# Attention quotients of two tiles at a time: four banks, one chain of VectorE operations per pair

## The chip, the cores and the metric

The kernel runs on one core of one Trainium2 chip. A core has TensorE (matmuls, PE in the profile), VectorE (DVE), ScalarE (ACT), GpSimd (POOL) and a queue for transfers on SyncE (SP). The engines run side by side and wait for each other through semaphores. PSUM, where matmuls put their results, is laid out by this kernel as eight banks. The metric is device time in microseconds (us), the median of several runs.

## The reference

It is a transformer block on 2048 rows of 448 features: a linear attention with 16 heads of 28 features, then a gated MLP.

```python
h  = x + A(layernorm(x));  h2 = h + B(layernorm(h))
# A, per head: phi(u) = [softmax(u @ w_phi), softmax(-u @ w_phi)]
kv  = einsum("bhsf,bhsd->bhfd", phi_k, v);  z = einsum("bhsf->bhf", phi_k)
num = einsum("bhqf,bhfd->bhqd", phi_q, kv)
den = einsum("bhqf,bhf->bhq", phi_q, z)[..., None] + 1e-6
o   = num / den                          # "the quotient"; then o @ wo
# B: (sigmoid(x @ w_gate) * (x @ w_up)) @ w_down
```

## The kernel before

The rows are 16 tiles of 128. A graph records every operation with what it reads and writes; ORDER lists, per engine, the order of the queue, and PROGRAM the order in which operations that share a bank follow one another. Semaphores are derived from both: a bank is written again only after the last reader of what it held. So a change of ORDER changes no arithmetic, only who waits for whom.

The quotient is worked by `num`. It already takes `n` tiles and a first bank `b`; each tile needs two banks. The kernel before always calls it with one tile.

```python
def num(t, n=1, b=6):
    s, NB = t % NS, 2 * n
    ...                                   # 16 small matmuls per tile into banks b, b+1, ...
    rsm = reciprocal(OM[..., E-1])        # VectorE, 16 numbers per row and tile
    qq  = rsm * OP[..., E-1]              # VectorE
    b   = OM[..., 0:EV] * qq              # VectorE, 464 numbers per tile, from PSUM
    c   = b + OP[..., 0:EV]               # VectorE, 464 numbers per tile, from PSUM
    den = 1e-6 * OP[..., E-1] + c[..., EV-1]   # VectorE, last reader of the banks
    rden = reciprocal(den)                # VectorE
    for each tile: o = c * rden           # GpSimd or VectorE, by ORDER; then a transpose
...
# kvz: the masked kv sums. Its columns of ones are copied beforehand, by VectorE or ScalarE, by ORDER:
cp(kvz[:, 0:2, ...] , maskK[...])         # 128 rows, 16 numbers, fp32 to bf16
for a, half in ((0, LO), (1, HI)):
    cp(kvz[half, 2, ...], maskK[half, a, ...])   # 64 rows, 8 numbers, twice
...                                       # whole code: cut here
```

(The code of `num` is abridged to its arithmetic; names are the kernel's. Others that come up below: phi of k is worked by ss (sums), rs (their reciprocals) and phi (the multiplication); v1 copies v out of PSUM; pq are the projections of q and eq their exps; oT is a quotient transposed, oTe its copy out of PSUM; h is the first residual sum, hn its layernorm, hT its transpose and hTe the copy of that which the gate matmuls, ga and gb, read; hh is the gated product. A number behind a name is the tile.)

The softmax here doesn't subtract the row's maximum and nothing guards it: scores larger than these inputs give would overflow.

## Time and profile before

| | before |
|---|---|
| median of three runs | 205.57 us |
| span of the profiled run | 203.7 us |
| TensorE busy | 97% of the span |
| VectorE busy | 67% |
| start of the first quotient matmul | 46.20 us |
| start of the first gate matmul | 61.01 us |

A line of a timeline reads: start, duration, engine, line of the code, operation, output and inputs, shapes, count, and in brackets how long the engine had been idle and what ended that. The stage at issue lies between the last two rows of the table: projections of q (with their exps on ScalarE), quotients, output projection and second layernorm of the first tiles, until the gate matmuls can start. After that TensorE runs nearly without holes to the end.

### The profile page before, as it was taken

How to read it: one execution, taken by the hardware profiler on the slowest of the kernel's cores; microseconds unless marked ns; L12 is line 12 of the kernel's file. 1: busy time of each engine (PE TensorE's matmuls, PEld its weight loads, DVE VectorE, ACT ScalarE, POOL GpSimd, SP SyncE). 2: the span in 40 equal slices, each digit the busy share in tenths (PEclk: the TensorE clock that was granted, in tenths of full speed). 3: DMA queues.
4: the chain of work that ended last, by engine and by line, in shares of the span. 5: the costliest groups of instructions: out<-in, count | busy, mean ns of one | idle time of the engine just before them, and what ended most of it. 6: DMA issues, size and time to landing. Idle time of an engine off the chain costs nothing.

```text
span 203.7 us, 5834 instructions
## 1 busy us (share of the span) xinstructions
PE 196.7 (97%) x2474; PEld 111.6 (55%) x2474; DVE 135.9 (67%) x340; ACT 97.4 (48%) x195; POOL 57.9 (28%) x98
## 2 busy tenths in 40 slices
PE   7899999999979999999999999999999999999995
PEld 3744556655448876777444544444555555554443
DVE  5899999978799988677668967526532422262224
ACT  2889999889892544522333343323522222222220
POOL 4699999942345310400023020001400000000000
PEclk9999999999999999999999999999999999999999
DMA  6975633899522371240004511040212000004002
GB/s 163 306 139 122 77 73 66 282 295 352 141 52 55 55 100 27 55 81 0 3 0 80 119 30 28 2 77 24 56 36 60 3 0 3 0 0 138 0 0 90
DMA packets 32866, 16.25 MB, mean 80 GB/s; under 512 B 25096, under 2 KB 31944, under 8 KB 32840
## 3 DMA queue, kind: packets, MB, share of 16 engines
q1 hardware_dynamic: 32336, 15.86, 33.2%
q8 instruction: 19, 0.31, 0.7%
q10 hardware_dynamic: 504, 0.03, 0.2%
q14 instruction: 7, 0.06, 0.1%
HBM read 8.34 MB, written 1.84 MB: 50 GB/s over the span
## 4 chain that ended last, share of the span: by engine, by line
PE 89%; DVE 4%; ACT 3%; DMA 1%; issue 1%; POOL 0%; DVEq 0%
PE psum L296 82%; PE psum L852 5%; DVE st L499 2%; DMA x_sb<-in_A_x_dram 1%; ACT eq L653 1%; ACT eq L652 1%; PE psum L567 1%; ACT junk L756 1%; ACT x_sb L748 1%; PE psum L492 1%; DVE kvz L683 1%; DVE mv L500 0%; DVE b_sb L717 0%; DVE c_sb L720 0%; POOL rst L512 0%
## 5 line engine op out<-in xcount | busy, mean ns | idle before, releaser
L296 PE MATMUL psum<-xnT,wg_sb 64*128 64x512 bf16 (+1 forms) x490 | 93.3, 333 | 0.4 <-ACT eq L653 0.2
L296 PE MATMUL psum<-xnT,wu_sb 64*128 64x512 bf16 (+1 forms) x490 | 93.0, 333 | 0.0
L824 ACT ACTIVATE sg_sb<-psum 128x512 bf16<-128x512 f32 (+1 forms) x70 | 35.0, 512 | 89.6 <-PE psum L296 89.0
L825 DVE SCALAR_TENSOR_TENSOR hhT<-sg_sb,psum 128x512 bf16<-128x512 bf16 (+1 forms) x70 | 39.0, 577 | 52.5 <-ACT sg_sb L824 52.1
L296 PEld LDWEIGHTS psum<-xnT,wg_sb 64*128 64x128 bf16 x490 | 44.3, 94 | 22.9 <-DVE hhT L825 4.8
L296 PEld LDWEIGHTS psum<-xnT,wu_sb 64*128 64x128 bf16 x490 | 44.3, 94 | 13.0
L296 PE MATMUL psum<-wd_sb,hhT 64*128 64x448 bf16 x336 | 36.9, 349 | 0.0
L296 PEld LDWEIGHTS psum<-wd_sb,hhT 64*128 64x128 bf16 x336 | 17.3, 94 | 14.8 <-DVE x_sb L751 0.6
L622 POOL TENSOR_TENSOR phi<-hhT,rs 128x896 bf16<-128x896 bf16 x14 | 24.1, 1738 | 0.9 <-PE psum L296 0.8
L296 PE MATMUL psum<-Wk,xnT 64*128 64x448 bf16 x112 | 22.3, 350 | 0.2
L296 PE MATMUL psum<-wv_sb,xnT 64*128 64x448 bf16 x112 | 22.4, 351 | 0.1
L759 POOL TENSOR_SCALAR ve<-ssq 128x1 f32<-128x1 f32 x16 | 3.1, 192 | 66.1 <-ACT junk L756 65.7
L618 DVE TENSOR_REDUCE ss<-hhT 128x32 f32<-128x896 bf16 x16 | 17.0, 1062 | 0.7 <-ACT hhT L615 0.7
L296 PE MATMUL psum<-xnT,Wq 64*120 64x512 bf16 x112 | 15.0, 385 | 0.1
L729 POOL TENSOR_TENSOR o_pad<-c_sb,rden 128x448 bf16<-128x448 bf16 x10 | 9.3, 936 | 15.6 <-DVE rden L725 13.4
L296 PE MATMUL psum<-wo_o,oT 64*128 64x448 bf16 x56 | 13.2, 350 | 0.0
L296 PE MATMUL psum<-wo_e,oT 64*128 64x448 bf16 x56 | 13.1, 349 | 0.0
L756 ACT ACTIVATE junk<-x_sb,nm 128x448 bf16<-128x448 bf16 x16 | 10.6, 661 | 1.9 <-DVE nm L754 1.8
L852 PE MATMUL psum<-wd_sb,hhT 128*128 128x448 bf16 (+2 forms) x70 | 11.1, 316 | 0.0
L859 DVE SCALAR_TENSOR_TENSOR x_sb<-psum,x_sb 128x448 bf16<-128x448 f32 (+2 forms) x17 | 9.4, 591 | 2.1 <-PE psum L852 1.6
L499 DVE BATCH_NORM_STATS2 st<-x_sb 128x6 f32<-128x448 bf16 x16 | 9.4, 611 | 1.9 <-DMA x_sb<-in_A_x_dram 1.9
L296 PEld LDWEIGHTS psum<-Wk,xnT 64*128 64x128 bf16 x112 | 7.6, 94 | 5.3 <-ACT hhT L615 0.7
(87 smaller groups left out, 240.3 us busy)
## 6 DMA issues: line engine op xcount, KB each, us to landing
out_dram<-x_sb SPq DMA_DIRECT2D x15, 112.0 KB, 1.8
x_sb<-in_A_x_dram SPq DMA_DIRECT2D x7, 224.0 KB, 4.5
wd_sb<-in_B_w_down_dram SPq DMA_DIRECT2D x7, 224.0 KB, 9.3
wg_sb<-in_B_w_gate_dram SPq DMA_DIRECT2D x3, 448.0 KB, 8.2
wu_sb<-in_B_w_up_dram SPq DMA_DIRECT2D x3, 448.0 KB, 6.9
wv_sb<-in_A_wqkv_dram SPq DMA_DIRECT2D x2, 224.0 KB, 5.0
wk_sb<-in_A_wqkv_dram SPq DMA_DIRECT2D x2, 196.0 KB, 3.3
wo_e<-in_A_wo_dram SPq DMA_DIRECT2D x1, 336.0 KB, 7.9
```

The source lines that it names most:

```text
L296: p = e.matmul(o, lhsT=w, rhs=r, start=st, stop=sp, tile_position=(row, 0))
L492: p = e.transpose(ps[:, kt * P:(kt + 1) * P], src, ident[:])
L499: op("dve", "bst%d" % t, lambda e: e.bn_stats(st1[:, t, :], x_sb[:, t, :]), r=[("x", t)], w=[("st1", t)])
L618: op("dve", "ss%d" % t, lambda e: e.tensor_reduce(ss[:, s, :], eks, AX.X, ALU.add), r=[("ek", s)], w=[("ss", s)])
L622: return e.tensor_tensor(phi[:, sp, :, :, :].rearrange("p b a n -> p (b a) n")[:, :, 0:56].rearrange("p b (h d) -> p b h d", h=2), eks.rea ...
L729: return e.tensor_tensor(o_pad[:, t % NO, off:off + D].rearrange("p (h d) -> p h d", h=H), c_sb[:, t % NS, :, 0:DH], rden[:, t % NS, :][:, ...
L756: op("act", "sq%d" % t, lambda e: e.activation(junk[:, t % 2, :], h_sb[:, t, :], ACT.Square, bias=nm2[:, t:t + 1], accum_out=ssq2[:, t:t + ...
L759: op("pool", "ve%d" % t, lambda e: e.tensor_scalar(ve2[:, t:t + 1], ssq2[:, t:t + 1], 1.0 / D, EPS, op0=ALU.mult, op1=ALU.add), r=[("ssq2" ...
L824: op("act", "sig" + nm, lambda e: e.activation(sg_sb[:, k, 0:N], bk(bg)[:, 0:N], ACT.Tanh, scale=0.5), r=[B(bg)], w=[("sg", k)])
L825: op("dve", "hh" + nm, lambda e: e.scalar_tensor_tensor(out=hhT[(t0 // 4) % NHH][:, ff, ns], in0=sg_sb[:, k, 0:N], scalar=1.0, in1=bk(bu)[ ...
L852: p = e.matmul(bk(b)[:, lo:hi], lhsT=hb[:, ff, TS(t)], rhs=wd_sb[:, ff, lo:hi], start=ff == 0, stop=ff == FT - 1)
L859: op("dve", "fin%d%s" % (t, nm), lambda e: e.scalar_tensor_tensor(out=h_sb[:, t, lo:hi], in0=bk(b)[:, lo:hi], scalar=0.5, in1=h_sb[:, t, l ...
```

## The change

The intent: an operation has a fixed cost; one operation over two tiles pays it once. So tiles 0 and 1 become one pair, tiles 2 and 3 another. A pair takes four banks in a row, 4 to 7, so the projections that used 4 and 5 have to go elsewhere. The queues were then put in a new order around this. The core of the diff:

```diff
 PROGRAM = (
-    "pq:0,0,4 pq:0,1,4 kvz pq:1,0,0 pq:1,1,4 pq:2,0,0 num:0 num:1,1,2 ot:0 ot:1 wo:0 pq:2,1,4 pq:3,0,0 num:2 "
-    "num:3 wo:2 pq:3,1,4 gu:0,2 num:4 ...
+    "pq:0,0,4 pq:0,1,4 kvz pq:1,0,0 pq:1,1,2 num:0,2,4 pq:2,0,0 ot:0 ot:1 wo:0 num:2,2,4 pq:2,1,0 wo:2 pq:3,0,0 "
+    "pq:3,1,4 gu:0,2 num:4 ...
 # ORDER, ScalarE: cuts marked ...
-    ... ek14 v1_14 ek15 kvzones v1_15 eq0_1 ... oT0e eq2_1 h1 h0 ...
+    ... v1_14 ek14 ek15 v1_15 eq0_1 ... oT0e oT1e eq2_1 h1 h0 ...
 # ORDER, VectorE
-    ... ss11 v1_12 rs11 phi10 ...
-    ... kvzA kvzD kvzC rsm0 qq0 b0 rsm1 c0 qq1 den0 b1 rden0 c1 rsm2 den1 qq2 rden1 b2 c2 den2 oT1e rsm3 ...
-    ... rsm5 qq5 b5 hn0 c5 hT1e den5 hT0e rden5 ...
+    ... ss11 kvzones v1_12 rs11 phi10 ...
+    ... kvzA kvzC kvzD rsm0 qq0 b0 c0 den0 rden0 o1 o0 rsm2 qq2 b2 c2 den2 rden2 rsm4 ...
+    ... rsm5 qq5 b5 hn1 c5 hn0 o4 den5 hT1e hT0e rsm6 rden5 ...
 # ORDER, TensorE
-    ... num0 num1 pqb1_1 pqa2_0 pqb2_0 num2 pqa2_1 oT0 pqb2_1 oT1 num3 woa0 wob0 num4 ...
+    ... num0 num1 pqb1_1 pqa2_0 pqb2_0 num2 num3 oT1 oT0 pqa2_1 pqb2_1 woa0 num4 wob0 ...
 # later stages, weight loads and GpSimd: reordered too, cut here
```

So besides the pairs, three things move between engines up to the gate: o0, o1 and o4 from GpSimd to VectorE, the ones of kvz ("kvzones") from ScalarE to VectorE, and one copy of a transpose (oT1e) from VectorE to ScalarE. (Later on, o10 and o11 change places between VectorE and GpSimd.)

## The prediction

> **What bounds the kernel now.** I read the page first. TensorE is busy for 97% of the span and the chain that ended last is 89% TensorE, so the time is TensorE's matmuls plus the holes between them.
>
> ```profile
> PE 196.7 (97%) x2474; PEld 111.6 (55%) x2474; DVE 135.9 (67%) x340; ACT 97.4 (48%) x195; POOL 57.9 (28%) x98
> PE 89%; DVE 4%; ACT 3%; DMA 1%; issue 1%; POOL 0%; DVEq 0%
> ```
>
> The change removes no matmul, so it can only open or close holes. TensorE's waits, longest first, show how little there is to close:
>
> ```profile
> PE psum L478 <- DVE zero L399: 1.2, 1, 1.2
> PE psum L492 <- DVE hn_pad L765: 0.6, 1, 0.6
> PE psum L296 <- DVE den L722: 0.6, 1, 0.6
> PE psum L296 <- DVE kvz L683: 0.5, 1, 0.5
> ```
>
> Line 478 is the warm-up. Between 45 us and the first gate matmul the timeline has holes after the kv masking (0.5), before the two hn transposes (0.6 and less), and before tile 6's quotient (0.57, for den). Adding small ones (starts of neighbouring matmuls further apart than the usual 0.19 to 0.23 us), I count about 3 us in 45 to 66 us, some of it semaphores that any order pays. After 66 us there are only three or four holes of 0.1 to 0.2 us. So the stage to look at ends where the gate matmuls begin:
>
> ```profile
> 60.41 0.40 PE L296 MATMUL psum<-kvz,eq 56*128 56x60 bf16 x16 [0.57 <-DVE den L722]
> 61.01 0.27 PE L296 MATMUL psum<-xnT,wg_sb 64*128 64x256 bf16 x1 [0.21 <-ACT eq L653]
> ```
>
> VectorE drives this stage: its timeline from 46.65 to 67.7 us has about 1 us idle. One serial chain (tile 6) and the groups by form give the costs:
>
> ```profile
> 60.85 0.26 DVE L714 RECIPROCAL rsm<-psum 128x16 f32<-128x16 f32 x1
> 61.14 0.17 DVE L715 TENSOR_TENSOR qq<-rsm,psum 128x16 f32<-128x16 f32 x1
> 61.35 0.64 DVE L717 TENSOR_TENSOR b_sb<-psum,qq 128x464 bf16<-128x464 f32 x1
> 62.02 0.64 DVE L720 TENSOR_TENSOR c_sb<-b_sb,psum 128x464 bf16<-128x464 bf16 x1
> 62.69 0.18 DVE L722 SCALAR_TENSOR_TENSOR den<-psum,c_sb 128x16 f32<-128x16 f32 x1
> ```
>
> ```profile
> L729 POOL TENSOR_TENSOR o_pad<-c_sb,rden 128x448 bf16<-128x448 bf16 x10 | 9.3, 936 | 15.6 <-DVE rden L725 13.4 <-DVE nm L754 2.0
> ...
> L619 DVE RECIPROCAL rs<-ss 128x32 f32<-128x32 f32 x16 | 5.3, 339 | 0.1
> ...
> L725 DVE RECIPROCAL rden<-den 128x16 f32<-128x16 f32 x16 | 3.8, 240 | 0.1
> L729 DVE TENSOR_TENSOR o_pad<-c_sb,rden 128x448 bf16<-128x448 bf16 x6 | 3.7, 622 | 0.1
> ```
>
> From start to next start: rsm 0.29, qq 0.21, b 0.67, c 0.67 us; den is 0.18 long. The last fence is from the groups by form: count, busy us, mean ns, idle before.
>
> **What the Trainium skill says.** "VectorE: DVE Perf Modes", sections "The TRN2 errata" and "The perf-mode tier table": a VectorE operation out of PSUM costs 120 + FD cycles at 0.96 GHz, and tensor_tensor with a PSUM operand runs at one element per cycle. For 464 elements that is 608 ns; the trace has 636 and 629, so it agrees within 5%. "PSUM — Partial Sum Buffer", section "PSUM bank collisions raise a hardware error": guard PSUM by bank. The kernel does, so a pair holds its four banks until the pair's last reader is done; the 0.57 us wait for den above is this guard for one tile. "GPSIMD Engine Reference", section 3 (its table of tensor_tensor): GpSimd takes 1.96 times VectorE's time for an fp32 add; here the o operation in bf16 takes 936 against 622 ns, 1.5 times, and the trace decides. "Perfetto Trace Analysis", "Identifying the Most-Contended Engine", calls matmul busy time a bad metric; hence I count holes between starts.
>
> **The change part by part.**
>
> 1. *Six VectorE operations per pair, not twelve.* The elements stay, the fixed parts halve. For b and c, 464 more elements at one per cycle are 0.483 us, so a pair's takes 0.67 + 0.48 = 1.15 start to start, against 1.34 for two. rsm and rden grow by about 0.10 (339 against 240 ns), qq and den by 0.02. The pair chain: rsm 0.39, qq 0.23, b 1.15, c 1.15, den 0.20 = 3.12 us to the release of the banks, then rden 0.39. Its length is about 3.5 us; before, tiles 0 and 1, interleaved so that each hides the other's latency, took 46.65 to 50.42 = 3.8 us. By pure busy time a pair saves some 0.9 us of VectorE, two pairs 1.8.
>
> 2. *Work moved onto VectorE.* o0, o1 and o4 come from GpSimd (3 x 0.62 = 1.86, start to start 1.6), the ones of kvz come from ScalarE (about 0.35), and oT1's copy leaves (0.4). Net, VectorE gains next to nothing before the gate stage.
>
> 3. *Four banks at once.* The pair uses banks 4 to 7, and both pairs the same four. Before, tile 2's matmuls started at 49.31 in banks 6 and 7 while tile 1 was still in 2 and 3. Now tiles 2 and 3 must wait for den of the first pair. This is the new wait.
>
> 4. *Query projections* of chunks 2 and 3 now go through banks 0 and 1 three times in a row, each after the exps of the one before (2 x 0.92 us on ScalarE).
>
> My walk, by the queue orders and the durations above:
> - The ones of kvz sit in a VectorE chain which GpSimd waits for (GpSimd's third phi from the end started at 38.16, right after the reciprocal that ended at 38.03), so the kv sums end about 0.2 us later: 46.2 becomes 46.4.
> - The rsm of the pair also waits for tile 1's matmuls (0.22): it starts at 47.07, den ends at 50.19. TensorE meanwhile has the two projections that end at about 49.5 and then stands for 0.7 us.
> - num 2 and 3: 50.25 to 50.75. o1 ends at 51.23, o0 at 51.77. The two transposes stand just behind in TensorE's queue, so it waits 0.5 and then 0.2 us more. oT0 ends at 52.15.
> - Projection 2_1 to 53.94; the wo matmuls of tile 0 to 54.9; den of the second pair (rsm 51.69, so 54.82) just in time for num 4; wo ends at 55.9. h1 on ScalarE starts at 56.15, against 54.73 before: 1.4 later.
> - hn1 came 2.88 us after h1's start (54.73 to 57.61), hn0 some 0.9 later: about 59.05 and 60.0. Then on VectorE's queue come o4 (0.54), den5, and the two copies of hnT: the last ends at about 61.7.
> - The first gate matmul starts at 61.8, against 61.01: **+0.8 us**. Its ten semaphore waits, which I think are the 0.37 us between copy and gate before, will partly have been passed already.
>
> What follows: num 7 waits for den 6 (about 0.35), but the hole of 0.3 at 65.45 before goes, since hh of the first gate tiles comes ahead. From there TensorE had almost no holes before, so a lag isn't made up, and weights are loaded long before they are used. I keep 0.8, nothing more and nothing back: 205.57 + 0.8 = **206.4 us**.
>
> **The rivals.**
>
> *The saved VectorE time shows up in full.* VectorE is nearly saturated in this stage, and 1.8 us less would close holes: 204 to 205 us. Against it: the moved o operations eat 1.6, and the four banks couple TensorE to the end of a longer chain. Also, two interleaved single chains hid latencies that a lone chain shows.
>
> *ScalarE becomes the bound.* Projections in banks 0 and 1 wait for the exps, and exp 3_1 ends at about 62.4, after the gate's start. The gate order was changed so that the tile in banks 0 and 1 goes first with both halves (0.8 us), which covers it. If h1 and its squares come later still, this would show as a wait for exp, and 207 to 207.5 us.
>
> *The lag is hidden.* If TensorE's holes of before (kv 0.5, hn 0.6 and 0.5, gate 0.2) are only exchanged for the new ones, since it now arrives later at the hn transposes, the time stays at 205.3 to 205.8. In my walk it does arrive late at hT1 (60.15) and hardly waits there; the 0.8 is what remains after that.
>
> *Later stages.* The reordered hh, nm and den operations could make gate tiles wait between 62 and 76 us: up to 1 us more.
>
> **Range and chances.** Runs of before differ by 0.5 us. My walk sums some 25 steps each good to 0.05 us, and one misjudged handover costs 0.3 to 0.5, so 205.5 to 207.6 should hold 8 in 10. Faster by over 2% needs 4.1 us out of holes that sum to 3 us: 1%. Slower by over 2% needs a new stall of 4.1 us, five times what I find: 3%. Else within 2%.
>
> **What would show it.** In the changed profile: a wait of TensorE for den of about 0.7 us near 49.5, one for o_pad's line on VectorE of 0.5 near 50.8; b and c of 928 elements at 1.10 to 1.13 us; the first gate matmul at 61.5 to 62.1. If b takes 0.9 or less, step 1 was mis-sized and the gate starts as early as before. If the kv masking isn't late, 0.2 of the loss falls away. If the gate starts at 61.8 but the end differs from +0.8 by over 0.5, the later stages decide, and my reading that lags stay is wrong.

## The result, and the profile after

The changed kernel took **207.65 us** (207.46 to 207.78, four runs), the kernel before in the same rounds 205.49. The ratio is 1.0103, with a 95% interval from 1.0083 to 1.0123: about 2.1 us slower. The change of 1% lies within 2%, as forecast, but the loss is 2.1 us against the 0.8 forecast, and 207.65 us lies just above the range of 205.5 to 207.6.

The engines' line on the page, and some of TensorE's waits, longest first (total, times, longest):

```profile
PE 197.4 (96%) x2474; PEld 110.1 (53%) x2474; DVE 138.0 (67%) x333; ACT 97.6 (47%) x193; POOL 55.5 (27%) x95
```

```profile
PE psum L296 <- DVE den L722: 0.9, 3, 0.5
PE psum L296 <- POOL phi L622: 0.6, 1, 0.6
...
PE psum L492 <- DVE o_pad L729: 0.4, 1, 0.4
```

The waits for den and for o_pad are the ones forecast (0.52 and 0.42 us where the forecast had 0.7 and 0.5). The wait for GpSimd's phi was not forecast: it belongs to the stage ahead of the quotients. TensorE's timeline shows where the time went. The first line is from the kernel before, the others are from the changed one:

```profile
46.20 0.63 PE L296 MATMUL psum<-kvz,eq 56*128 56x60 bf16 x32 [0.49 <-DVE kvz L683]
```

```profile
47.73 0.63 PE L296 MATMUL psum<-kvz,eq 56*128 56x60 bf16 x32 [0.43 <-DVE kvz L683]
...
51.58 0.63 PE L296 MATMUL psum<-kvz,eq 56*128 56x60 bf16 x32 [0.52 <-DVE den L722]
52.63 0.93 PE L492 MATMUL psum<-ident,o_pad 128*128 128x128 bf16 x8 [0.42 <-DVE o_pad L729]
...
63.16 0.27 PE L296 MATMUL psum<-xnT,wg_sb 64*128 64x256 bf16 x1 [0.41 <-DVE rsm L714]
```

The first quotient starts at 47.73 against 46.20, 1.5 us late, before a single pair has been worked. From there to the first gate matmul it takes 15.43 us, against 14.81 before: 0.6 us more. So the larger part of the loss arises ahead of the pairs. The same stage in the kernel before, VectorE first, then the ones on ScalarE:

```profile
34.41 0.63 DVE L485 CAST v<-psum 128x448 bf16<-128x448 f32 x1 [0.15 <-PE psum L296]
```

```profile
41.08 0.27 ACT L426 CAST kvz<-maskK 128x16 bf16<-128x16 f32 x1
41.18 0.46 ACT L429 CAST kvz<-maskK 64x8 bf16<-64x8 f32 x2
```

In the changed kernel, VectorE's timeline and then GpSimd's show the cause:

```profile
33.41 1.03 DVE L618 TENSOR_REDUCE ss<-hhT 128x32 f32<-128x896 bf16 x1
34.36 1.57 DVE L426 CAST kvz<-maskK 128x16 bf16<-128x16 f32 x1
35.82 0.36 DVE L429 CAST kvz<-maskK 64x8 bf16<-64x8 f32 x2
36.20 0.63 DVE L485 CAST v<-psum 128x448 bf16<-128x448 f32 x1
...
37.12 1.03 DVE L622 TENSOR_TENSOR phi<-hhT,rs 128x896 bf16<-128x896 bf16 x1
```

```profile
34.18 1.70 POOL L622 TENSOR_TENSOR phi<-hhT,rs 128x896 bf16<-128x896 bf16 x1 [0.38 <-PE psum L296]
37.29 2.41 POOL L622 TENSOR_TENSOR phi<-hhT,rs 128x896 bf16<-128x896 bf16 x1 [1.41 <-DVE rs L619]
```

The first copy of the ones, 16 numbers per row, is on record with 1.57 us; its two smaller sisters take 0.18 each. It ends at 35.93, as GpSimd's multiplication (34.18 plus 1.70) ends at 35.88. (GpSimd's durations in a profile are rough; this one fits the spacing of such multiplications where they follow one another, 3.35 us for two.) Then everything behind it is late: the evacuation of v at 36.20 (34.41 before), the reciprocal, and with it GpSimd's next phi, idle for 1.41 us "<-DVE rs". Note that nothing is shown as idle on VectorE: the wait sits inside the copy's own duration. It is to be found only by asking why one operation takes eight times what its shape takes elsewhere (1.57 us, against 0.19 in e4 below).

The lag is then handed on through GpSimd. Its next phi starts 1.18 us later than in the kernel before (37.29 against 36.11), and lasts 2.41 us in place of 2.09, where the other phis take about 1.7: it ends at 39.70 against 38.20, 1.5 us late, which is the lateness of the first quotient. VectorE multiplies from 37.12 to 38.15 meanwhile, so here GpSimd seems to be the one that is held up; no run was made to test that.

The pair operations themselves, from the groups by form:

```profile
L717 DVE TENSOR_TENSOR b_sb<-psum,qq 128x928 bf16<-128x928 f32 x2 | 2.2, 1124 | 0.1
L720 DVE TENSOR_TENSOR c_sb<-b_sb,psum 128x928 bf16<-128x928 bf16 x2 | 2.2, 1120 | 0.1
```

### The profile page after: what moved, and what is told of

Same layout as the page of the kernel before. It is cut to its first block, busy times and chain, and to the rows that moved or that the text cites. A ratio compares the mean times of both kernels' runs of the same rounds, so it can differ in the third digit from the quotient of the medians.

```text
span 206.0 us, 5822 instructions
## 1 busy us (share of the span) xinstructions
PE 197.4 (96%) x2474; PEld 110.1 (53%) x2474; DVE 138.0 (67%) x333; ACT 97.6 (47%) x193; POOL 55.5 (27%) x95
## 4 chain that ended last, share of the span: by engine, by line
PE 79%; DVE 10%; ACT 4%; DMA 2%; issue 2%; POOL 1%; SPq 1%
PE psum L296 73%; PE psum L852 5%; DMA x_sb<-in_A_x_dram 2%; DVE ss L618 2%; DVE b_sb L717 1%; POOL phi L622 1%; DVE c_sb L720 1%; SPq L395 1%; ACT hhT L614 1%; DVE v L485 1%; DVE o_pad L729 1%; ACT hhT L615 1%; ACT v L485 1%; ACT xn_pad L525 1%; DVE kvz L683 1%
## 5 line engine op out<-in xcount | busy, mean ns | idle before, releaser
L729 POOL TENSOR_TENSOR o_pad<-c_sb,rden 128x448 bf16<-128x448 bf16 x7 | 6.5, 936 | 34.5 <-DVE rden L725 34.5
```

Source lines behind the costliest of these rows:

```text
L729: return e.tensor_tensor(o_pad[:, t % NO, off:off + D].rearrange("p (h d) -> p h d", h=H), c_sb[:, t % NS, :, 0:DH], rden[:, t % NS, :][:, ...
```

## The experiments

Eleven kernels ran, each in five rounds, against the kernel before on the same chip. Its median was 205.35 us in the rounds of the e and g runs, 205.57 in those of the f runs and c1, so between these groups the ratios compare better than the medians. Two of the six of f1 took 208.5 and 208.9 us without a cause that the record shows, which lifts its ratio.

| run | what | median us | ratio to before | 95% interval |
|---|---|---|---|---|
| (changed kernel) | | 207.65 | 1.0103 | 1.0083 to 1.0123 |
| e1_ones_act | changed, ones on ScalarE | 206.26 | 1.0045 | 1.0032 to 1.0057 |
| e2_before_ones_dve | before, ones on VectorE | 206.94 | 1.0077 | 1.0064 to 1.0090 |
| e3_ones_reduce | changed, ones as a reduction | 206.20 | 1.0041 | 1.0027 to 1.0055 |
| e4_ones_idle | changed, ones later on VectorE | 206.22 | 1.0041 | 1.0028 to 1.0053 |
| f1_o01_gpsimd | e1, o0 and o1 on GpSimd | 207.12 | 1.0100 | 1.0070 to 1.0131 |
| f2_singles_same_banks | e1, pairs taken apart | 206.35 | 1.0040 | 1.0027 to 1.0053 |
| f3_o4_gpsimd | e1, o4 on GpSimd | 206.61 | 1.0052 | 1.0039 to 1.0065 |
| g4_half_first_pair | e1, half of b and c, pair 1 | 205.94 | 1.0026 | 1.0014 to 1.0039 |
| g3_half_second_pair | e1, half of b and c, pair 2 | 206.20 | 1.0043 | 1.0031 to 1.0056 |
| g5_o4_behind_copies | e1, o4 behind the copies | 206.17 | 1.0039 | 1.0025 to 1.0052 |
| c1_before_gate_sooner | before, gate sooner | 206.05 | 1.0026 | 1.0013 to 1.0040 |

### Is it the ones? Undo that part, and do it alone

The theory: GpSimd's multiplication held up VectorE's copy. The Trainium skill, "SBUF — State Buffer", section "Who interferes with whom", says that a copy or cast on VectorE can run in a mode that takes a pair of SBUF ports shared with GpSimd, that whoever issues first has it for the whole instruction, and that the other "fully blocks". A reduction on VectorE never takes it, by the same section.

e1 puts the ones back where the kernel before has them:

```diff
-dve: ... ss11 kvzones v1_12 ...        act: ... ek15 v1_15 ...
+dve: ... ss11 v1_12 ...                act: ... ek15 kvzones v1_15 ...
```

> The changed kernel, but the ones of kvz go back to ScalarE, where the kernel before has them. Theory: VectorE's first copy of the ones lost 1.4 us to GpSimd (it took 1.57 us in the changed kernel's trace, the two that follow 0.17 each), and that is the part of the loss that I missed. Then the kv masking starts about 1.2 us earlier than in the changed kernel and the time is 206.2 to 206.5, so 0.6 to 0.9 over before. Rival A (the four banks and the longer chain cost the whole 2.1 us, the late masking is hidden behind VectorE's work): 207.3 or more. Rival B (all of the loss is the ones): 205.5.

Measured 206.26 us, inside the theory's range; rivals A and B both fall. In its profile the first quotient starts at 46.17 and the first gate matmul at 61.63. By ratios the ones cost 0.0058 of 205.4, so 1.2 us (1.4 by medians), and 0.9 us remain.

```profile
46.17 0.63 PE L295 MATMUL psum<-kvz,eq 56*128 56x60 bf16 x32 [0.43 <-DVE kvz L682]
...
61.63 0.27 PE L295 MATMUL psum<-xnT,wg_sb 64*128 64x256 bf16 x1 [0.44 <-DVE rsm L713]
```

e2 does that part alone, in the kernel before:

```diff
-dve: ... ss11 v1_12 ...                act: ... ek15 kvzones v1_15 ...
+dve: ... ss11 kvzones v1_12 ...        act: ... ek15 v1_15 ...
```

> The kernel before, and only the ones of kvz move from ScalarE to VectorE, at the place where the changed kernel has them. Theory: the copy again waits for GpSimd's multiplication, the masking is 1.0 to 1.4 us late, and since VectorE drives the stage up to the gate matmuls the time rises by about as much: 206.4 to 206.9. Rival A: hidden, 205.4 to 205.8.

Measured 206.94, 1.6 us over the kernel before (1.3 to 1.9 by the interval), a little above the range. VectorE's timeline has the same line as the changed kernel:

```profile
34.14 1.56 DVE L426 CAST kvz<-maskK 128x16 bf16<-128x16 f32 x1
35.59 0.36 DVE L429 CAST kvz<-maskK 64x8 bf16<-64x8 f32 x2
```

The first quotient starts at 47.47 and the gate at 62.28, both 1.27 late. So no slack takes it back, in either kernel.

### Is it the port, the place or the copy?

e3 leaves the ones at the same place in the queue, and changes only the kind of operation. A first version of it, with a sum, did not build (the builder refuses a sum that accumulates in bf16); a maximum over an axis of length one gives the same numbers.

```diff
-op(("dve", "act"), "kvzones", (kvzones(lambda e: e.tensor_copy), ...
+op(("dve", "act"), "kvzones", (kvzones(lambda e: lambda d, m: e.tensor_reduce(d, m[..., None], AX.X, ALU.max)), ...
```

> The changed kernel, with the three copies of the ones at the same place on VectorE, but issued as a maximum over an axis of length one, which the Trainium skill (SBUF, Who interferes with whom) says never shares a port with GpSimd. Theory of the shared port: each takes 0.15 to 0.3 us, and the time falls to 206.2 to 206.7, within 0.3 of the run with the ones on ScalarE. Rival (the place in VectorE's queue or the strided pattern is what costs): the first one still takes over 1 us and the time stays at 207.4 to 207.8.

```profile
34.09 0.44 DVE L434 TENSOR_REDUCE kvz<-maskK 128x16 bf16<-128x16 f32 x3
```

```profile
33.93 1.70 POOL L624 TENSOR_TENSOR phi<-hhT,rs 128x896 bf16<-128x896 bf16 x1 [0.40 <-PE psum L296]
```

All three together take 0.44 us, while GpSimd multiplies from 33.93 to 35.63, and the time is 206.20. Same place, same addresses, same patterns, no block: neither the place nor the pattern costs. The cost lies in the kind of operation.

e4 keeps the copies, and moves them to where GpSimd has nothing to do:

```diff
-dve: ... ss11 kvzones v1_12 ... phi15 kvzA ...
+dve: ... ss11 v1_12 ... phi15 kvzones kvzA ...
```

> The changed kernel, with the same copies on VectorE moved behind the last phi, where VectorE idles for 0.8 us waiting for TensorE and GpSimd's last phi has ended. Theory: the first copy takes 0.2 us, nothing is late, 206.2 to 206.5, as with the ones on ScalarE. Rival (the copy is slow by itself): 1.5 us there too, and the masking is 1 us late: 207.3 or more.

```profile
43.98 0.19 DVE L425 CAST kvz<-maskK 128x16 bf16<-128x16 f32 x1
44.06 0.36 DVE L428 CAST kvz<-maskK 64x8 bf16<-64x8 f32 x2
```

The very same copy takes 0.19 us, and the time is 206.22. So it is the meeting of this kind of operation with GpSimd's multiplication. With e1 to e4 the larger part of the loss is settled. That the thing shared is a port is what the skill's page says; the runs show the blocking, not the port.

### The remaining 0.9 us: pairs, banks, or the moved quotients?

All that follow, except c1, start from e1 (ones on ScalarE, 206.26 us).

f2 takes the pairs apart: tile 0 in banks 4 and 5, tile 1 in 6 and 7, then 2 and 3 likewise, VectorE's operations interleaved as in the kernel before. (The two transposes swap places, as o0 now comes first.)

```diff
-PROGRAM: num:0,2,4 ... num:2,2,4
+PROGRAM: num:0,1,4 num:1,1,6 ... num:2,1,4 num:3,1,6
-dve: rsm0 qq0 b0 c0 den0 rden0 o1 o0 rsm2 qq2 b2 c2 den2 rden2
+dve: rsm0 qq0 b0 rsm1 c0 qq1 den0 b1 rden0 c1 den1 o0 rden1 o1 rsm2 qq2 b2 rsm3 c2 qq3 den2 b3 rden2 c3 den3 rden3
```

> The changed kernel with the ones on ScalarE, and the pairs taken apart: twelve VectorE operations for two tiles, interleaved as in the kernel before, in the same banks 4 to 7 and the same order of everything else. Theory (a pair's chain is as long as two interleaved ones, 3.5 against 3.8 us, so pairing itself gives and costs almost nothing here): 206.1 to 206.7. Rival A (the lone chain with its exposed handovers is the loss): 205.6 or less. Rival B (pairing saves 0.9 us of VectorE per pair in full): 207.3 or more.

Measured 206.35: the same within the noise. Pairing as such gives nothing and costs nothing here that these runs can tell. Tile 2's matmuls, which no longer wait for the whole first pair, start at 49.34 as before (49.31), and yet the gate starts no sooner (61.74). What remains must come from the order and the banks around it.

f1 gives o0 and o1 back to GpSimd:

```diff
-dve: ... rden0 o1 o0 rsm2 ...          pool: ... phi14 o2 o3 ...
+dve: ... rden0 rsm2 ...                pool: ... phi14 o1 o0 o2 o3 ...
```

> The changed kernel with the ones of kvz on ScalarE (206.26 us), and the quotients o0 and o1 back on GpSimd. Theory: the rest of the loss, 0.9 us, comes from the order that the four banks force (quotients, transposes, output projection one behind the other), so o1 and o0 at 0.94 us each on GpSimd make the transposes 0.3 and 0.8 us later, the output projection 0.5 later, and the time 206.5 to 206.9. Rival (the 1.1 us that o0 and o1 take of VectorE are the loss): the second pair starts 1.1 us sooner and the time falls to 205.3 to 205.7.

```profile
51.54 0.40 PE L491 MATMUL psum<-ident,o_pad 128*128 128x128 bf16 x4 [0.77 <-POOL o_pad L728]
52.43 0.40 PE L491 MATMUL psum<-ident,o_pad 128*128 128x128 bf16 x4 [0.50 <-POOL o_pad L728]
```

Measured 207.12. The direction is the theory's, and the median lies above its range; in these rounds the kernel before was slower by 0.2 us as well, so against it f1 loses 0.6 us more than e1. The second transpose starts at 52.43 against 51.61 in e1, and the gate at 62.43 against 61.63. Counted from the first quotient (46.28 against 46.17) both are 0.7 late: I had thought that part would be hidden, and none is. Taking 1.1 us off VectorE did not help, delaying o0 hurt in full. So o0 lies on the path that sets the gate.

g4 and g3 take VectorE's work away on that path and off it. They give wrong results: b and c of one pair cover half of their elements.

```diff
+m = NB // 2 if t == 0 else NB          # g4; g3: if t == 2
-b: out=h3(b_sb), in0=OMv[..., 0:EV], ...
+b: out=h3(b_sb)[:, 0:m], in0=OMv[:, 0:m, :, 0:EV], ...        # c likewise
+dve: one memset of c's unwritten half, in idle time at the start
```

> Wrong results on purpose. The changed kernel with the ones on ScalarE (206.26 us), and b and c of the first pair worked for half of their elements only, so VectorE saves 0.97 us ahead of o1 and o0 (a memset of 464 elements is added in VectorE's idle time at the start). Theory: what is left of the loss sits on the line first pair, o1 and o0, transposes, projection, output projection, h1, hn, gate; the transposes come 0.9 us sooner, the projection behind them then waits for the exps of the one before (51.4), and the gate starts about 0.5 sooner: 205.6 to 205.9. Rival (no part of that line binds): 206.1 to 206.4.

> Wrong results on purpose. The same with the second pair instead of the first: VectorE saves the same 0.97 us, but off the line named there. Theory: hn1 and hn0 wait for the output projection and ScalarE, so nothing moves, 206.0 to 206.4. Rival (VectorE's throughput up to the gate binds, whatever is removed): 205.2 to 205.5.

g3 measured 206.20: VectorE sheds 0.97 us in the second pair and nothing moves; it then idles 1.14 us for TensorE. g4 measured 205.94, 0.3 to 0.4 us better, just over the upper end of its range. From first quotient to gate g4 takes 15.04 us (46.49 to 61.53), e1 15.46, g3 15.43. And g4's next hole is the one foretold, the projection in banks 0 and 1 waiting for the exps:

```profile
50.42 0.93 PE L492 MATMUL psum<-ident,o_pad 128*128 128x128 bf16 x8
51.86 1.56 PE L295 MATMUL psum<-xnT,Wq 64*120 64x512 bf16 x9 [0.51 <-ACT eq L653]
```

So VectorE's throughput does not bind this stage as a whole. What f1, g3 and g4 fit is one line of dependences: first pair, o1 and o0, transposes, projection, output projection, hn, gate. Two steps that ran beside each other before (tile 2's quotients, and the projection in banks 4 and 5) stand in a row on it.

### Three attempts to win some of it back

At the end of the line, o4 stands on VectorE ahead of the two copies that release the gate. f3 gives o4 back to GpSimd:

```diff
-dve: ... hn0 o4 den5 hT1e hT0e ...     pool: ... pow2_0 o5 ...
+dve: ... hn0 den5 hT1e hT0e ...        pool: ... pow2_0 o4 o5 ...
```

> The changed kernel with the ones on ScalarE, and the quotient o4 back on GpSimd. In VectorE's queue o4 stands ahead of den5 and of the two copies that release the gate matmuls. Theory: the gate starts 0.4 to 0.5 us sooner, at 61.1 to 61.3, and the time is 205.7 to 206.0. Rival (what follows is bound by VectorE anyway and takes it back): 206.1 to 206.4 with the gate early and a new hole after it.

Measured 206.61, a miss for both theory and rival. By ratios it is 0.1 us slower than e1, which the intervals don't separate, but the forecast gain is not there: from first quotient to gate it takes 15.67 us (46.19 to 61.86), e1 15.46. The two timelines, VectorE's and GpSimd's, tell why:

```profile
58.81 0.41 DVE L764 TENSOR_SCALAR hn_pad<-x_sb,nm,rst 128x512 bf16<-128x512 bf16 x1
...
59.72 1.02 DVE L764 TENSOR_SCALAR hn_pad<-x_sb,nm,rst 128x512 bf16<-128x512 bf16 x1
```

```profile
59.66 0.94 POOL L728 TENSOR_TENSOR o_pad<-c_sb,rden 128x448 bf16<-128x448 bf16 x1
```

The same operation hn takes 0.41 us alone, and 1.02 when GpSimd's o4 starts 0.06 us ahead of it; it ends at 60.74, o4 at 60.60. It looks like the block of e1 to e4 again, on another operation. Moving o4 frees VectorE of 0.54 us and costs hn0 0.6.

g5 leaves o4 on VectorE but behind den6:

```diff
-dve: ... hn0 o4 den5 hT1e hT0e rsm6 ... den6 hh0_1
+dve: ... hn0 den5 hT1e hT0e rsm6 ... den6 o4 hh0_1
```

> The changed kernel with the ones on ScalarE, and o4 on VectorE moved from before den5 and the two copies of hnT to behind den6 (GpSimd is idle at hn0, so unlike the run with o4 on GpSimd nothing can hold hn0). Theory: the copies end 0.4 to 0.5 us sooner, the gate starts at 61.1 to 61.2; VectorE then is no further behind with den6, so 205.7 to 206.0. Rival (hh and the quotients after the gate take it back): 206.1 to 206.4.

Measured 206.17, the rival's range: first quotient to gate shrinks by 0.23 only, as the copies now wait for the transposes, and of that about 0.1 us is left in the time, which is within the noise.

c1 is the kernel before with the gate started sooner:

```diff
-pe:  hT1 hT0 num6 ga0_1 ga0_0 gb0_1 ...     dve: hn1 rsm5 qq5 b5 hn0 c5 hT1e den5 hT0e rden5
+pe:  hT1 hT0 ga0_1 gb0_1 num6 ga0_0 ...     dve: hn1 rsm5 qq5 hn0 b5 hT1e hT0e c5 den5 rden5
```

> Not an undoing but an attempt at a better kernel: the kernel before, with the second hn operation ahead of b5 and the two copies of hnT ahead of c5 on VectorE, and the first gate tile ahead of tile 6's quotient on TensorE. Theory: the holes before the second transpose and before tile 6 close, the gate starts at 60.2 to 60.5 and the time is 204.8 to 205.1. Rival (VectorE, which has no idle time here, takes it back after the gate has started): 205.2 to 205.7.

The gate did start at 60.36 in place of 61.01, and the time rose to 206.05, past even the rival's range. TensorE then has a new wait for den of 0.36 us at 63.89 and a hole before 66.60. So an earlier start of the next stage gained nothing; that the chains behind it came later is my reading of these two holes. None of these kernels beats the kernel before; it stays the fastest.

## Why the prediction was wrong

- **The step that failed** is the first of the walk: "The ones of kvz sit in a VectorE chain which GpSimd waits for [...] so the kv sums end about 0.2 us later", from a cost of "about 0.35" for the copies. The place was right and so was the mechanism of handing the delay on. The size was wrong: the copies took 1.8 us (34.36 to 36.18), the first quotient started 1.5 us late in the changed kernel and 1.27 in e2, not 0.2. The cost was about right for copies that nobody holds up: in e4 all three take 0.44 us (43.98 to 44.42). What was left out is the wait for GpSimd's multiplication, which e3 and e4 show by taking it away.
- **The sum without that term holds up to the gate.** The forecast has 0.6 us from pairs and banks besides the 0.2. e1, without the late ones, has the gate at 61.63 against 61.01, 0.62 later, and a time 0.9 us over; the forecast had 0.6 for both.
- **The walk through the pairs holds within 0.1 us at the steps checked**, counted from the first quotient. TensorE's second pair of matmuls: forecast 3.85 us later, measured 3.85. Transposes: 4.88 and 4.90. First gate matmul: 15.4 and 15.43. b and c: 1.12 long, forecast 1.10 to 1.13. The waits for den and o_pad show as shorter than forecast, but the starts after them agree.
- **Which rival came true.** None of those listed. "The saved VectorE time shows up in full" is refuted by f2 and g3. "ScalarE becomes the bound" is not seen at the gate; ScalarE shows up only once the first pair is made shorter, in g4. "The lag is hidden" is refuted by the 0.6. "Later stages" cost some 0.2 to 0.3 us: e1's loss of time is 0.9 for a gate 0.62 late.
- **One reading was half right**: "VectorE drives this stage". It is busy nearly throughout, but g3 shows that taking 1 us of its work away need not move anything. Being busy and being on the path are two things.
- **Left open**: why some 0.2 us more are lost after the gate. The profiled spans grow by 0.8 us in e1, 1.5 in e2 and 2.3 in the changed kernel, and the gates come 0.62, 1.27 and 2.15 later. How the 0.6 divides is settled only in part. In g4 the first pair's chain no longer holds up the projection, which waits for the exps instead, and 0.2 us of the 0.6 are still there (15.04 us from first quotient to gate, against 14.81 in the kernel before). So some 0.4 go with the first pair's chain; the rest stays with the bank plan and the new order, which no run takes apart.

## What to carry to other kernels

Before moving even a tiny operation between engines, look at what the neighbouring engine does at that time: a copy of 16 numbers cost 1.2 to 1.6 us, because it is of a kind that waits on VectorE while GpSimd multiplies, and the profile shows that as a long operation and not as a wait. Joining operations saves their fixed costs only where the engine's time is on the path; here it saved nothing, while the plan of banks and queues made for the joined chains put steps in a row that had run side by side.

## What the Trainium skill lacked or had wrong

- "SBUF — State Buffer", section "Who interferes with whom": these runs agree with it, and it would have corrected the forecast. What it lacks is how this looks in a profile when VectorE is the one that waits: the blocked operation's own duration grows (1.57 us for a copy that takes 0.19; 1.02 for an hn that takes 0.41), VectorE shows no idle time, and the end falls 0.05 to 0.14 us after the end of GpSimd's operation.
- "Perfetto Trace Analysis", section "Per-instruction lifecycle", lists waits that fall outside the reported duration. It doesn't name this one, which falls inside it (1.57 us against 0.19).
- "VectorE: DVE Perf Modes", section "The TRN2 errata": an estimate from its formula, 120 + 928 cycles at 0.96 GHz for b of a pair, is 1092 ns, and 1124 were measured, 3% more; the one-tile form is also some 5% over. A small correction.
- "GPSIMD Engine Reference", section 3: 1.96 times VectorE's time, for 2048 fp32 numbers; the bf16 quotients here, 448 numbers, take 936 against 622 ns, 1.5 times. The page has no figure for bf16.
